# First chunk's diagonals by halves of 256 tokens, in a fused convolution and swish layer on one NeuronCore

## The chip, the cores and the metric

The kernel runs on one core of a Trainium2 chip. The metric is the device time of one execution in microseconds (us). Engines: PE is TensorE, with PEld its weight loads; DVE is VectorE; ACT is ScalarE; POOL is GpSimd; SP is SyncE, which here only issues DMAs.

## What is computed

```python
w = softmax(weight, axis=-1)                       # 8 heads x 7 taps
x_pad = zeros(6 tokens) ++ x                       # x: 8 x 4096 x 192, float32
a[b, s, h, g] = sum_k w[h, k] * x_pad[b, s + k, h, g]    # causal convolution, 24 channels a head
h = a.reshape(32768, 192) @ w_in                   # 192 x 2048
g = h * sigmoid(beta * h)                          # beta: 2048
out = g @ w_out                                    # 2048 x 192, float32
```

The kernel leaves the factor 1/beta to w_out: it computes silu(beta*h) and scales w_out's rows by 1/beta.

## The kernel before

**Tiling.** Channels lie on partitions, tokens along the free dimension. The 192 channels make three groups (index `c` or `j`, 0 to 2) of 64, and two batches are stacked, so a tile has 128 partitions: 64 channels of batch p and 64 of batch p+4. A chunk is 512 tokens (`TOK`), four blocks of 128; there are 32 chunks (`s`). `xt` is a chunk of x transposed, with a halo of earlier tokens in front; `ct` is the convolved chunk. For each chunk, 16 hidden blocks (`u` or `fc`) of 128 features follow: `hidden` multiplies w_in with ct on TensorE (L429), six matmuls of 64 rows, ScalarE applies silu (L437) into `g`. `output` (L511) multiplies g with w_out in pairs of matmuls (L465), accumulated over all 16 blocks in a PSUM tile; VectorE adds its two halves (L483), and SP writes them out.

**Order.** Each engine executes its instructions in the order in which the program issues them. The order is written by hand: what is called earlier stands earlier in its engine's queue. PSUM has three pools: `psum_h` with two buffers of two banks (tile `ph`), `psum_a` and `psum_b` with one each (`pa`, `pb`, from `in_a()` and `in_b()`). A new tile from a pool waits until the readers of the old one are done. Waits between engines follow from the tiles that instructions read and write.

**The start (chunk 0).** Weights and x are loaded in pieces by SP, ScalarE and POOL queues. `fill` (L215) issues matmuls of zeros whose result nobody reads. The softmax gives `cw`, the seven tap weights of each channel; `diags` (L255) makes diagonal matrices of them on VectorE, so that a tap of the convolution is a matmul with a diagonal. At L302 to L307 the four blocks b of chunk 0, cast to bf16 (L221), are transposed on TensorE (L228) and evacuated to `xt0`, by VectorE for b = 2 and by ScalarE for the others (L305); a fill follows b = 1 and b = 3. Then beta is transposed (L311) and copied (L312). At L340 the taps come as diagonal matmuls of 512 columns (`diag_tap`, L290): group 2 with three taps, group 0 with seven, group 1 with seven. VectorE adds the last four taps of group 2 (L328); ScalarE evacuates groups 0 and 1 (L345, L347), with the cast of w_in's first 256 columns between (L346), after it has cast half of the second chunk, `x1b` (L343).

**The second chunk.** `second()` (L365) transposes x1b with 24 small matmuls into a PSUM tile (L373), which VectorE copies to `xt1` and `xt` (L383). `conv1` (L394) makes group 0 of chunk 1 by diagonal matmuls at u = 4 and 5, evacuated by VectorE at u = 6 (L407); its other groups are VectorE's (L326, L328).

**Weights.** POOL issues w_in in quarters (L206). The last is issued after the first scaling of w_out on POOL (L316), which needs w_out's first quarter and `beta_r`, the reciprocal of beta (L359).

Of the kernel before, what the change touches and what calls it, by code (L numbers as in the profile page):

```python
# [9 lines left out]
FP32 = mybir.dt.float32  # L10
FP32R = mybir.dt.float32r
BF16 = mybir.dt.bfloat16
# [5 lines left out]
def kernel(  # L18
# [17 lines left out]
    nc = tc.nc  # L36

    B, S, D = x.shape
    H, K = weight.shape
    F = moe_w_in.shape[1]  # L40
    group = D // H
    DG = 64
    NG = D // DG
    HP = group // NG
    TOK = 512
    NF = F // 128
    PAD = K - 1
    HALO = 16
# [7 lines left out]
    NB = TOK // BLK  # L56
# [12 lines left out]
    psum_h = ctx.enter_context(  # L69
        tc.tile_pool(name="psum_h", bufs=2, space=bass.MemoryType.PSUM)  # L70
    )
# [9 lines left out]
    def in_a():  # L81
        return psum_a.tile([128, 2, TOK], FP32, name="pa")

    def in_b():
        return psum_b.tile([128, 2, TOK], FP32, name="pb")
# [25 lines left out]
    def new_xt(ch):  # L111
        xt = xt_pool.tile([128, NG, HALO + TOK], BF16, name="xt")
        xts[ch] = xt
        return xt
# [37 lines left out]
    beta_q = setup.tile([NF, 128], FP32)  # L152
# [15 lines left out]
    for r in range(2):  # L168
# [8 lines left out]
    xt0 = setup.tile([128, NG, HALO + TOK], FP32R)  # L177
# [9 lines left out]
        fill=0.0,  # L187
# [8 lines left out]
        fill=0.0,  # L196
# [18 lines left out]
    def fill(n, cols=TOK):  # L215
        zc = zeros.unsqueeze(1).to_broadcast((128, cols // 128, 128))
        for _ in range(n):
            nc.tensor.matmul(pf[:, 0, 0:cols], zeros, zc, start=True, stop=True)  # L218
# [36 lines left out]
    def diags(k0, k1):  # L255
        nc.vector.tensor_tensor(
            diag[:, k0:k1],
            ident.unsqueeze(1).to_broadcast((128, k1 - k0, 128)),
            cw[:, k0:k1].unsqueeze(2).to_broadcast((128, k1 - k0, 128)),
            ALU.mult,  # L260
        )
# [21 lines left out]
    cts = {}  # L283

    def new_ct(s):
        cts[s] = ct_pool.tile([128, NG, TOK], BF16, name="ct")

    def diag_tap(k, xt, pv, rows=slice(0, 128), k1=K):
        o = HALO - PAD + k
        nc.tensor.matmul(  # L290
            pv,
            diag[rows, k, :],
            xt[rows, o : o + TOK],
            start=(k == 0),
            stop=(k == k1 - 1),
        )
# [5 lines left out]
    for b in range(NB):  # L302
        pt = pts[b % 3][:, b // 3, 0 : NG * BLK].rearrange("p (c q) -> p c q", c=NG)
        transposes(pt, x0b, b)
        (nc.vector.tensor_copy if b == 2 else nc.scalar.copy)(tokens(xt0, b), pt)  # L305
        if b % 2:
            fill(1, 512 if b > 1 else 256)  # L307
    diags(2, 4)
    diags(4, K)
    pb = pf[:, 1, 0:NF]  # L310
    nc.tensor.transpose(pb, beta_q, ident[0:NF, 0:NF])  # L311
    nc.scalar.copy(beta, pb)  # L312

    def scale_w_out(i):
        fcs = slice(i * NQ, (i + 1) * NQ)
# [7 lines left out]
    def tap(dst, src, k, added):  # L323
# [6 lines left out]
            )  # L330


    new_ct(0)
    K_P = 3
    pvs = [
        psum_h.tile([128, 2, TOK], FP32, name="ph")[:, 0, :],
        in_b()[:, 0, :],
        in_a()[:, 0, :],
    ]
    for c, k1 in (2, K_P), (0, K), (1, K):  # L340
        for k in range(k1):
            diag_tap(k, xt0[:, c], pvs[c], k1=k1)
    for b in range(2):  # L343
        cast_rows(nc.scalar.copy, x1b, x1, b)
    nc.scalar.copy(cts[0][:, 0, :], pvs[0])  # L345
    nc.scalar.copy(w_in_s[:, :, 0:F0], w_in_raw)  # L346
    nc.scalar.copy(cts[0][:, 1, :], pvs[1])  # L347
    dst = cts[0][:, 2, :]
    for k in range(K_P, K):
        o = HALO - PAD + k  # L350
        tap(
            dst,
            xt0[:, 2, o : o + TOK].bitcast(FP32),
            k,
            pvs[2] if k == K_P else dst,
        )
    for b in range(2, NB):
        cast_rows(nc.vector.tensor_copy, x1b, x1, b)
# [3 lines left out]
    scale_w_out(1)  # L362


    def second():  # L365
        xt = new_xt(1)
        pt = in_b().bitcast(BF16)
        for b in range(NB):
            for c in range(NG):
                for r in range(2):  # L370
                    rows = slice(r * DG, (r + 1) * DG)
                    o = ((b // 2 * NG + c) * 2 + b % 2) * DG
                    nc.tensor.transpose(  # L373
                        pt[:, r, o : o + DG],
                        x1b[rows, b, c].rearrange("q h p -> q (h p)"),
                        ident_b[rows, rows],
                    )
        head, tail = slice(HALO - PAD, HALO), slice(HALO + TOK - PAD, HALO + TOK)
        nc.vector.tensor_copy(xt1[:, head], xt0[:, 0, tail])
        nc.vector.tensor_copy(xt[:, 1:, head], xt0[:, 1:, tail])  # L380
        for c in range(NG):
            dst = xt[:, c, HALO:] if c else xt1[:, HALO:]
            nc.vector.tensor_copy(  # L383
                dst.rearrange("p (i r q b) -> p i r q b", i=2, r=2, b=2),
                pt[:, :, 0 : NB * NG * DG].rearrange(
                    "p r (i c b q) -> p i r c q b", i=2, c=NG, b=2
                )[:, :, :, c],
            )
# [5 lines left out]
    def conv1(k0, k1):  # L394
        if not conv1_ps:
            new_ct(1)
            conv1_ps.append(in_b())
        pv = conv1_ps[0]
        for k in range(k0, k1):
            for r in range(2):  # L400
                diag_tap(k, xt1, pv[:, r, :], slice(r * DG, (r + 1) * DG))

    def conv1_evac():
        pv = conv1_ps[0]
# [16 lines left out]
    def hidden(s, fc, js=range(NG), ph=None, last=NG - 1):  # L421
        if fc == 0 and s not in gs:
            gs[s] = g_pool.tile([128, NF, 2, TOK], BF16, name="g")
        if ph is None:
            ph = psum_h.tile([128, 2, TOK], FP32, name="ph")
        for j in js:
            for h in range(2):
                rows = slice(h * DG, (h + 1) * DG)
                nc.tensor.matmul(  # L429
                    ph[:, h, :],  # L430
                    w_in_s[rows, j, fc * 128 : (fc + 1) * 128],
                    cts[s][rows, j, :],
                    start=(j == 0),
                    stop=(j == last),
                )
            if j == last:
                nc.scalar.activation(  # L437
                    gs[s][:, fc], ph, AF.Silu, scale=beta[:, fc : fc + 1]
                )
        return ph  # L440
# [70 lines left out]
    def output(s, u, pairs, free):  # L511
        for _ in range(pairs):
            for name in free:
                if slots[name] is None and waiting:
                    slots[name] = waiting.popleft()

            live = [(j.s, j.h, j.q, n) for n, j in slots.items() if j is not None]
            for *_, name in sorted(live):
                job = slots[name]
                if job.ready(s, u):  # L520
                    break
            else:
                return
            if job.po is None:
                job.po = place[name]()
            if job.pair():
                job.leave()
                slots[name] = None
# [22 lines left out]
    for s in range(N_ST):  # L551
        jobs_of(s)
        for u in range(NF):
            if s == 0 and u == min(CONV1):
                conv1(0, 2)
            if s > 0 or u > 2:
                hidden(s, u)
            elif u == 0:
                ph = hidden(0, 0, (0, 2), last=1)
                ph1 = hidden(0, 1, [0], last=1)  # L560
                hidden(0, 0, [1], ph, last=1)
                second()
                hidden(0, 1, (2, 1), ph1, last=1)
            elif u == 2:
                hidden(0, u, ph=in_a())
            if s > 0:
                n = 6 if s == N_ST - 1 else 4 if s == 1 and u == 0 else 8
                output(s, u, n, "ab")
            elif u > 7:
                output(s, u, 5 if u < NF - 1 else 10, "ab")  # L570
            elif u in QUOTA_A:
                output(s, u, QUOTA_A[u], "a")
            if s == 0:
                if u in CONV1:
                    conv1(*CONV1[u])
                if u == min(CONV1):
                    queue.extend(conv_ops(1, 1))
                for work in first_work.get(u, []):
                    (work or queue.popleft())()
            else:  # L580
                if u % 2 and queue and (s, u) != (1, 1):
                    queue.popleft()()

                if u == 0 and s + 3 < N_CH:
                    load(s + 3)
                if u < 2 and s + 2 < N_CH:
                    cast(s + 2, u)
                if u == 1 and s + 2 < N_CH:
                    xpose(s + 2)
                if (s, u) == (1, 1):  # L590
                    queue.popleft()()
            if u == 12 and s + 2 < N_CH:
                queue.extend(conv_ops(s + 2, 0))
# [32 lines left out]
```

## Time and profile before

| | us |
|---|---|
| median of 5 runs | 689.39 |
| lowest and highest | 689.14, 690.8 |
| the profiled execution: time | 690.8 |
| the profiled execution: span from first to last instruction | 689.0 |
| PE busy | 683.6 (99%) |
| ACT busy | 577.9 (84%) |
| DVE busy | 524.3 (76%) |
| POOL busy | 10.7 (2%) |

Times in the profile count from the span's start. A timeline row has start, length, engine, line, operation and tiles, and in square brackets the idle time of the engine before it with what ended the wait. Where a row stands for several instructions (x7), its length reaches from the first's start to the last's end. The end of a matmul is modelled and lies behind the start of the next; the pace is read from start to start.

### The profile page before, as it was taken

What the parts mean: (1) busy time and instruction counts of PE and PEld (TensorE: products, weight loads), DVE (VectorE), ACT (ScalarE), POOL (GpSimd) and SP (SyncE); (2) the same over time, 40 slices, a digit from 0 to 9 for tenths busy, and PEclk for the clock granted to TensorE, in tenths of its full rate; (3) what the DMA queues carried; (4) which work ended last, traced back from release to release, by engine and by line L of the source; (5) the groups of instructions that cost most, each with busy time, mean ns of one, the idle gap of its engine ahead of it and who ended that gap; (6) DMA issues with size and microseconds to landing.
All of it is one profiled execution on the core that took longest, in us unless ns stands there. A gap on an engine that the chain in (4) does not pass through costs nothing.

```text
span 689.0 us, 24342 instructions
## 1 busy us (share of the span) xinstructions
PE 683.6 (99%) x11312; PEld 520.2 (76%) x11312; DVE 524.3 (76%) x466; ACT 577.9 (84%) x529; POOL 10.7 (2%) x21
## 2 busy tenths in 40 slices
PE   9999999999999999999999999999999999999998
PEld 5777777777777777777777777777777777777777
DVE  6888877788777797777787777887777977777712
ACT  7888888888888888888888888888888888888893
POOL 4100000000000000000000000000000000000000
PEclk9999999999999999999999999999999999999999
DMA  9754332244332343332344332443324433322111
GB/s 232 178 110 117 105 99 85 64 116 116 94 104 67 88 116 105 100 103 56 104 117 105 95 85 67 116 117 93 105 65 89 117 106 99 97 62 59 49 36 59
DMA packets 121861, 67.06 MB, mean 97 GB/s; under 512 B 53264, under 2 KB 121760, under 8 KB 121760
## 3 DMA queue, kind: packets, MB, share of 16 engines
q1 hardware_dynamic: 120048, 64.12, 34.5%
q0 software_dynamic: 1664, 1.38, 1.2%
q8 instruction: 88, 1.44, 0.9%
q14 instruction: 13, 0.11, 0.0%
q10 hardware_dynamic: 48, 0.01, 0.0%
HBM read 29.89 MB, written 25.17 MB: 80 GB/s over the span
## 4 chain that ended last, share of the span: by engine, by line
PE 96%; DMA 3%; POOL 1%; DVE 0%; ACT 0%; issue 0%; POOLq 0%
PE ph L429 47%; PE pa L465 25%; PE pb L465 24%; DMA w_out_raw<-in_moe_w_out_dram 1%; DMA w_in_s<-in_moe_w_in_dram 1%; POOL w_in_s L206 0%; PE ph L218 0%; POOL w_out_s L316 0%; PE pa L239 0%; ACT cw L246 0%; ACT osb L481 0%; POOL hold L270 0%; DVE cw L249 0%; DVE nmax L245 0%; DVE total L248 0%
## 5 line engine op out<-in xcount | busy, mean ns | idle before, releaser
L437 ACT ACTIVATE g<-ph,beta 128x1024 bf16<-128x1024 f32 x511 | 568.5, 1114 | 95.4 <-PE ph L429 91.1
L465 PEld LDWEIGHTS <-g 64*128 64x128 bf16 x8160 | 369.9, 94 | 104.1 <-issue 0.9
L429 PE MATMUL ph<-ct,w_in_s 64*128 64x512 bf16 x3066 | 423.5, 376 | 0.2 <-DMA w_in_s<-in_moe_w_in_dram 0.2
L328 DVE SCALAR_TENSOR_TENSOR ct<-xt,cw,ct 128x1536 bf16<-128x1536 bf16 (+2 forms) x189 | 338.3, 1790 | 2.5
L465 PE MATMUL pa<-w_out_s,g 64*128 64x192 bf16 x4112 | 244.3, 243 | 0.1
L465 PE MATMUL pb<-w_out_s,g 64*128 64x192 bf16 (+1 forms) x4048 | 230.1, 243 | 0.3 <-DVE ct L407 0.3
L429 PEld LDWEIGHTS <-w_in_s 64*128 64x128 bf16 x3072 | 158.8, 94 | 54.7 <-issue 1.0
L483 DVE TENSOR_REDUCE osb<-pa 128x384 f32<-128x768 f32 x64 | 61.3, 958 | 122.9 <-PE pa L465 122.9
L483 DVE TENSOR_REDUCE osb<-pb 128x384 f32<-128x768 f32 x63 | 60.3, 958 | 29.0 <-PE pb L465 29.0
L106 DVE CAST xb<-xf 128x768 bf16<-128x768 f32 x60 | 40.6, 678 | 0.0
L326 DVE TENSOR_SCALAR ct<-xt,cw 128x1536 bf16<-128x1536 bf16 (+1 forms) x31 | 30.7, 990 | 0.0
L481 ACT COPY osb<-pb 128x192 f32<-128x192 f32 x1 | 0.3, 318 | 7.2 <-PE pb L465 7.2
L218 PE MATMUL ph<-zeros 128*128 128x512 bf16 (+2 forms) x10 | 4.5, 575 | 1.1 <-DVE warm L175 1.1
L206 POOL DMA_DIRECT2D w_in_s<-in_moe_w_in_dram x8 | 5.2, 657 | 0.0
L290 PE MATMUL pb<-xt,diag 64*128 64x512 f32 (+1 forms) x21 | 4.4, 437 | 0.3 <-DVE xt L383 0.3
L121 DVE COPY xt<-xt 128x18 bf16<-128x18 bf16 x27 | 4.4, 163 | 0.0
L316 POOL TENSOR_TENSOR w_out_s<-w_out_raw,beta_r 128x768 bf16<-128x768 f32 x2 | 3.9, 1926 | 6.7 <-DMA w_out_raw<-in_moe_w_out_dram 6.6
L290 PEld LDWEIGHTS pb<-xt,diag 64*128 64x128 f32 (+1 forms) x21 | 2.7, 187 | 1.3 <-PE ph L429 0.8
L218 PEld LDWEIGHTS <-zeros 128*128 128x128 bf16 x10 | 1.2, 134 | 2.2 <-issue 1.1
L176 ACT ACT_TABLE_LOAD x1 | 1.3, 1283 | 1.8 <-issue 1.8
L316 DVE TENSOR_TENSOR w_out_s<-w_out_raw,beta_r 128x768 bf16<-128x768 f32 x2 | 1.9, 943 | 0.0
L290 PE MATMUL ph<-xt,diag 128*128 128x512 f32 x7 | 1.8, 394 | 0.0
(59 smaller groups left out, 30.1 us busy)
## 6 DMA issues: line engine op xcount, KB each, us to landing
out_dram<-osb SPq DMA_DIRECT2D x127, 192.0 KB, 2.2
xf<-in_x_dram SPq DMA_DIRECT2D x60, 384.0 KB, 4.3
xt<-xb SPq DMA_TRANSPOSE x120, 2.5
x<-in_x_dram SPq DMA_DIRECT2D x4, 384.0 KB, 4.7
w_out_raw<-in_moe_w_out_dram SPq DMA_DIRECT2D x4, 384.0 KB, 11.3
w_in_s<-in_moe_w_in_dram POOLq DMA_DIRECT2D x6, 192.0 KB, 8.2
w_in_raw<-in_moe_w_in_dram SPq DMA_DIRECT2D x2, 192.0 KB, 6.7
w_in_s<-in_moe_w_in_dram POOLq DMA_DIRECT2D x2, 96.0 KB, 6.4
```

The lines of the kernel that those rows point to most:

```text
L106: nc.vector.tensor_copy(xbs[ch][:, :, :, h, :], xfs[ch][:, h].rearrange("q b (p c) -> q b c p", c=NG),)
L121: nc.vector.tensor_copy(dst, last[:, :, HALO + TOK - PAD :])
L206: nc.gpsimd.dma_start(out=w_in_s[r * DG : (r + 1) * DG, :, c0:c1], in_=w_in_v[:, :, c0:c1])
L218: nc.tensor.matmul(pf[:, 0, 0:cols], zeros, zc, start=True, stop=True)
L290: nc.tensor.matmul(pv, diag[rows, k, :], xt[rows, o : o + TOK], start=(k == 0), stop=(k == k1 - 1),)
L316: (nc.vector if i > 1 else nc.gpsimd).tensor_tensor(w_out_s[:, fcs, :], w_out_raw[:, fcs, :], beta_r[:, fcs].unsqueeze(2).to_broadcast((12 ...
L326: nc.vector.tensor_scalar_mul(dst, src, scalar)
L328: nc.vector.scalar_tensor_tensor(out=dst, in0=src, scalar=scalar, in1=added, op0=ALU.mult, op1=ALU.add)
L429: nc.tensor.matmul(ph[:, h, :], w_in_s[rows, j, fc * 128 : (fc + 1) * 128], cts[s][rows, j, :], start=(j == 0), stop=(j == last),)
L437: nc.scalar.activation(gs[s][:, fc], ph, AF.Silu, scale=beta[:, fc : fc + 1])
L465: nc.tensor.matmul(self.po[:, r, b * D : (b + 1) * D], g[rows, fc, self.h, q * BLK : (q + 1) * BLK], w_out_s[rows, fc, :], start=(self.don ...
L483: nc.vector.tensor_reduce(dst, self.po[:, :, 0 : nb * D].rearrange("p r n -> p n r"), axis=mybir.AxisListType.X, op=ALU.add,)
```

## The change

- The taps of groups 0 and 1 are made together, by halves of 256 tokens: one matmul has both groups' 256 tokens as its 2x256 columns. The order is four taps of half 0, three taps of group 2, three taps of half 0, seven of half 1. Half 0 goes to the unused second bank of the tile that took block 1's transposes.
- The evacuations change with it: half 0 for both groups in one copy, half 1 in two, one for each group.
- Beta's transpose and its copy, and `diags(2, 4)`, move to behind block 1's; both fills in the loop go.
- `second` is called in two parts: blocks 0 and 1 ahead of the first hidden matmuls, 2 and 3 where it was.
- PSUM pools a and b swap their roles for the second chunk's transposes, conv1, the hidden block u = 2 and the first output job.

```diff
-    def diag_tap(k, xt, pv, rows=slice(0, 128), k1=K):
-        o = HALO - PAD + k
+    def diag_tap(k, pv, moving, rows=slice(0, 128), k1=K):
         nc.tensor.matmul(
             pv,
             diag[rows, k, :],
-            xt[rows, o : o + TOK],
+            moving,
...
         (nc.vector.tensor_copy if b == 2 else nc.scalar.copy)(tokens(xt0, b), pt)
-        if b % 2:
-            fill(1, 512 if b > 1 else 256)
-    diags(2, 4)
+        if b == 1:
+            pb = pf[:, 1, 0:NF]
+            nc.tensor.transpose(pb, beta_q, ident[0:NF, 0:NF])
+            nc.scalar.copy(beta, pb)
+            diags(2, 4)
     diags(4, K)
-    pb = pf[:, 1, 0:NF]
-    nc.tensor.transpose(pb, beta_q, ident[0:NF, 0:NF])
-    nc.scalar.copy(beta, pb)
...
     K_P = 3
-    pvs = [
-        psum_h.tile([128, 2, TOK], FP32, name="ph")[:, 0, :],
-        in_b()[:, 0, :],
-        in_a()[:, 0, :],
-    ]
-    for c, k1 in (2, K_P), (0, K), (1, K):
-        for k in range(k1):
-            diag_tap(k, xt0[:, c], pvs[c], k1=k1)
+    HT = TOK // 2
+    halves = [pts[1][:, 1].bitcast(FP32), in_b()[:, 0, :]]
+    pv2 = in_a()[:, 0, :]
+
+    def half_taps(i, k0, k1):
+        for k in range(k0, k1):
+            o = HALO - PAD + i * HT + k
+            diag_tap(
+                k,
+                halves[i].rearrange("p (c t) -> p c t", c=2),
+                xt0[:, 0:2, o : o + HT],
+            )
+
+    def half_evac(i, c0, c1):
+        nc.scalar.copy(
+            cts[0][:, c0:c1, i * HT : (i + 1) * HT],
+            halves[i].rearrange("p (c t) -> p c t", c=2)[:, c0:c1],
+        )
+
+    half_taps(0, 0, 4)
+    for k in range(K_P):
+        o = HALO - PAD + k
+        diag_tap(k, pv2, xt0[:, 2, o : o + TOK], k1=K_P)
+    half_taps(0, 4, K)
+    half_taps(1, 0, K)
     for b in range(2):
         cast_rows(nc.scalar.copy, x1b, x1, b)
-    nc.scalar.copy(cts[0][:, 0, :], pvs[0])
+    half_evac(0, 0, 2)
     nc.scalar.copy(w_in_s[:, :, 0:F0], w_in_raw)
-    nc.scalar.copy(cts[0][:, 1, :], pvs[1])
+    half_evac(1, 0, 1)
+    half_evac(1, 1, 2)
...
-    def second():
-        xt = new_xt(1)
-        pt = in_b().bitcast(BF16)
-        for b in range(NB):
+    pt1 = in_a().bitcast(BF16)
+
+    def second(b0, b1):
+        pt = pt1
+        for b in range(b0, b1):
...
+        if b1 < NB:
+            return
+        xt = new_xt(1)
...
             elif u == 0:
+                second(0, 2)
                 ph = hidden(0, 0, (0, 2), last=1)
                 ph1 = hidden(0, 1, [0], last=1)
                 hidden(0, 0, [1], ph, last=1)
-                second()
+                second(2, NB)
                 hidden(0, 1, (2, 1), ph1, last=1)
             elif u == 2:
-                hidden(0, u, ph=in_a())
+                hidden(0, u, ph=in_b())
```

More of the change, by code (lines that the diff above doesn't have):

```diff
@@ L354 @@
             k,
-            pvs[2] if k == K_P else dst,
+            pv2 if k == K_P else dst,
         )
@@ L396, in conv1 @@
             new_ct(1)
-            conv1_ps.append(in_b())
+            conv1_ps.append(in_a())
         pv = conv1_ps[0]
         for k in range(k0, k1):
+            o = HALO - PAD + k
             for r in range(2):
-                diag_tap(k, xt1, pv[:, r, :], slice(r * DG, (r + 1) * DG))
+                rows = slice(r * DG, (r + 1) * DG)
+                diag_tap(k, pv[:, r, :], xt1[rows, o : o + TOK], rows)
     def conv1_evac():
@@ L571 @@
             elif u in QUOTA_A:
-                output(s, u, QUOTA_A[u], "a")
+                output(s, u, QUOTA_A[u], "b")
             if s == 0:
```

## The prediction

> **What bounds the kernel now.** I read the page's busy table first: TensorE is busy for 683.6 of 689.0 us, so only time that TensorE loses can be won, some 5 us in all, nearly all of it before 27 us. The change touches only the first 16 us; behind it the built program is the same instruction for instruction, but for two PSUM buffers that swap roles. So the question is which wait ends last between 0 and 27 us. The chain of waits that ended last, in order of time (start, length, what), answers it:
>
> ```profile
> 6.43 8.78 DMA w_out_raw<-in_moe_w_out_dram
> ...
> 15.38 1.49 POOL w_out_s L316
> 16.87 0.62 POOL w_in_s L206
> 17.49 8.49 DMA w_in_s<-in_moe_w_in_dram
> 25.98 0.05 issue
> 26.02 0.69 PE ph L429 x5
> ```
>
> The last quarter of w_in is queued on POOL behind the first scaling of w_out, which waits for a load; it lands at 25.98, and from then on TensorE runs without a gap. None of the taps, transposes or evacuations that the change edits is in this chain. The timeline (start, length, instruction, idle before it and its releaser) shows how near they are to it:
>
> ```profile
> 6.51 0.63 PE L218 MATMUL ph<-zeros 128*128 128x512 bf16 x1
> ...
> 6.75 0.51 ACT L305 CAST xt<-pb 128x384 fp32r<-128x384 bf16 x1 [0.41 <-PE pb L228]
> ...
> 7.31 1.13 PE L290 MATMUL pa<-xt,diag 128*128 128x512 f32 x3
> ...
> 8.28 1.79 PE L290 MATMUL ph<-xt,diag 128*128 128x512 f32 x7
> 8.57 0.75 DVE L328 SCALAR_TENSOR_TENSOR ct<-xt,cw,pa 128x512 bf16<-128x512 f32 x1 [0.79 <-PE pa L290]
> 9.35 2.33 DVE L328 SCALAR_TENSOR_TENSOR ct<-xt,cw,ct 128x512 bf16<-128x512 f32 x3
> ...
> 11.72 0.58 ACT L347 CAST ct<-pb 128x512 bf16<-128x512 f32 x1 [0.29 <-PE pb L290]
> ...
> 12.85 2.12 ACT L437 ACTIVATE g<-ph,beta 128x1024 bf16<-128x1024 f32 x2 [0.54 <-PE ph L429]
> ...
> 23.04 0.42 PE L465 MATMUL pb<-w_out_s,g 64*128 64x192 bf16 x6 [0.26 <-DVE ct L407]
> ...
> 25.40 0.38 PE L429 MATMUL ph<-ct,w_in_s 64*128 64x512 bf16 x1
> ...
> 26.02 0.82 PE L429 MATMUL ph<-ct,w_in_s 64*128 64x512 bf16 x5 [0.25 <-DMA w_in_s<-in_moe_w_in_dram]
> ```
>
> The two row halves of a hidden matmul run side by side. At u = 12 the first starts at 25.40 and its partner only at 26.02. So the front has **0.62 us of cover**: what it gains up to there is lost in this wait, and what it loses costs nothing until 0.62 us are used up.
>
> **The change, part by part**, on the times of this execution.
>
> Does the half start early? The new first matmul reads tokens of blocks 0 and 1 only (evacuated by 6.34). But in the built program it carries a wait for ScalarE's seventh count, which is the evacuation of block 3, and for VectorE's copy of block 2; the group that needs these blocks carries none of its own. Block 3's evacuation is the row at 6.75 and ends at 7.26. So the first tap starts at **7.31 as before**. The two fills go (0.21 and 0.43 us of columns at the cold rate) and leave TensorE idle from 6.6 to 7.31. Beta's transpose (0.28) and copy (0.17) move into ScalarE's idle 0.41 us before block 3: nothing. diags(2,4) ahead of block 2's copy shifts VectorE by 0.42 us at 6.2, inside waits: nothing.
>
> Taps: 17 before, 3+7+7; 17 after, 4+3+3+7. A tap of 2x256 columns is not in the trace: at least the 0.233 us from start to start of the 7 rows at 8.28 ((1.79-0.39)/6), at most twice a 256-column fill's pace, which is the same columns. I take 0.233. The third tap of group 2 comes four taps later: 8.05+4x0.233 = 8.98, and VectorE's first tap moves 8.57 to **9.50**, its fourth ends at 12.61 instead of 11.68. Half 0 is complete after ten taps, as group 0 was; its evacuation and the w_in cast stay at 10.11 and 10.59, and the last tap stays at 11.30. Half 1's two evacuations of 128x256 on ScalarE: between the 0.17 us of 16 columns and the 0.58 of 512, by width 0.37 each. c0 is then whole at 12.09 (10.69 before), c1 at about 12.4 (12.30).
>
> First hidden matmuls: before, the last pair started at 12.36, waiting for c1. After: j=0 at 12.1, j=2 waits for VectorE until 12.68, two more pairs of 0.216: 13.11. The first activation goes from 12.85 to **13.60**, and the next five stand back to back behind it, so ScalarE is 0.75 late until its seventh (19.24).
>
> Second chunk: 12 of the 24 transposes (0.17 of 0.34 us) run at 11.5 while TensorE waits anyway. The others follow the late hidden pair, 13.33 to 13.50 (x1b's cast, late with the taps, ends at 13.27). VectorE's copies move 13.14 to 13.72, **+0.58**. Behind them VectorE is busy without a break until conv1's evacuation; TensorE's wait for that (0.26 at 23.04) absorbs part of its lateness. TensorE, 0.65 behind and 0.26 of it regained, reaches u = 12 at about 25.8: 0.4 of the 0.62 is used. The end moves by 0.0 to 0.1. beta_r moves to 13.4, and w_out's scaling waits for its load until 15.23: 1.8 us of cover. SP's queue and POOL's keep their order.
>
> [...] POOL's scalings take 1.49 and 2.36 us for the same work, and in the same stretch three VectorE taps take 6.09 where others take 1.28 each. [...] Before, L326 (15.06 to 15.55) was ahead of the scaling at 15.38. [...] I take +0.1 for the end and keep -0.2 and +0.4 for the range.
>
> [...] The trace's clock record begins at 7.70 us; before, the fills start 0.43 us apart (1.89 for four at 1.06), later taps 0.233. [...] By the rows alone, the clock comes at 7.7 and the sum is +0.1. [...] nine taps at 0.427. Then the group-2 taps end the wait of VectorE at 10.65, its taps end at 13.76; the last tap starts at 12.79; the last hidden pair at 14.25 (+1.89); the first activation at 14.73; VectorE's copies at 14.86 (+1.73). TensorE is 1.8 late, regains the 0.26 at 23.04, and comes to u = 12 at 25.40+1.54 = 26.94 with no DMA left to wait for: its next pair at 26.96 instead of 26.02, **+0.94**. beta_r at 14.57 is still ahead of 15.23.
>
> **Rivals and their times.** The profiled execution was timed at 690.8 with a span of 689.0; the median of the runs is 689.39. I put the shift on the median. 0.2% of it is 1.38 us, about what can be told from no change.
>
> - The forecast: [...] no visible change, 689.39+0.94 = **690.3**. [...] Chance 0.40, its own range 689.9 to 690.7.
> - The clock on time, +0.1: 689.5, chance 0.29. For it: by instruction records TensorE is rarely idle; against it: the 0.7 us gap before 7.31.
> - The other side, slower: [...] From 11.1 on every us that it is late costs half a us, so +1.38 is reached at 12.0, and 13.4 gives +2.1. Place: TensorE's taps and first hidden matmuls, with no cover left. 691.1 in the middle, chance 0.25.
> - Earlier: [...] w_in lands 0.2 to 0.4 sooner, with the front no later than now: 689.1, chance 0.06. More can't come of it, since TensorE itself reaches u = 12 at 25.40. That the halves do start early (a wait ending at 6.6 instead of 7.31) is inside this: the gain would go into the same DMA wait.
>
> Slower than 0.2%: 0.25 of the third, some of the first's edge and of a later landing: 0.31. Faster: 0.03. The same: 0.66. The range 689.0 to 691.5 leaves out the ends of the third and fourth.
>
> **What would show it.** The first tap at 7.31 with nothing on TensorE for 0.7 us before it; VectorE's first tap at 9.5 (clock on time) or 10.6 (late); taps 0.43 apart beyond 7.7; the first activation at 13.6 or 14.7; the wait for w_in at u = 12 shrunk to 0.2 or gone; POOL's w_in issue within 0.4 of 16.87. I am wrong if the first tap starts near 6.6, if the load lands over 1 us away from 25.98, or if a difference arises behind 27 us.

## The result and the profile after

The changed kernel takes a median of 690.26 us over 22 runs (689.74 to 692.31), the kernel before 689.73 over 42 runs (689.10 to 691.0). The ratio is 1.0013 with a 95% interval of 1.0007 to 1.002: the change costs about 0.9 us. The medians alone differ by 0.53, the means (690.75 and 689.82) by 0.93, because the changed kernel's runs fall into two groups: 12 lie between 689.74 and 690.38, 10 between 691.35 and 692.31, and none between. The profiled execution is of the second group: 691.71 us with a span of 690.0, 1.0 more than the span before.

Its chain of waits (start, length, what) is shown from block 3's evacuation to the first output matmuls in PSUM pool a. It no longer holds a DMA:

```profile
6.74 0.52 ACT xt L304
...
7.30 2.08 PE ph L289 x4
9.38 1.29 PE pa L289 x3
...
10.77 0.76 DVE ct L326
...
13.93 0.82 PE ph L452 x6
14.76 0.19 PE pa L391 x12
...
14.97 1.90 DVE xt L404 x3
...
16.89 2.45 DVE ct L324
...
24.64 0.42 PE pa L488 x6
```

It goes from ScalarE's evacuation over the taps to VectorE's taps, from there over the first hidden matmuls and the second chunk's transposes to VectorE's copies, and through VectorE's queue to the output. The timeline of the same execution gives the rows that answer to those of before:

```profile
6.21 0.50 PE L228 MATMUL pb<-ident_b,x0b 128*128 128x128 bf16 x3
...
7.30 2.08 PE L289 MATMUL ph<-xt,diag 128*128 128x512 f32 x4 [0.60 <-ACT xt L304]
...
9.18 1.48 PE L289 MATMUL pa<-xt,diag 128*128 128x512 f32 x3
...
10.77 0.75 DVE L326 SCALAR_TENSOR_TENSOR ct<-xt,cw,pa 128x512 bf16<-128x512 f32 x1 [3.32 <-PE pa L289]
...
14.84 1.47 POOL L314 TENSOR_TENSOR w_out_s<-w_out_raw,beta_r 128x768 bf16<-128x768 f32 x1 [6.05 <-DVE beta_r L376]
14.85 2.12 ACT L460 ACTIVATE g<-ph,beta 128x1024 bf16<-128x1024 f32 x2 [1.18 <-PE ph L452]
14.97 0.69 DVE L404 CAST xt<-pa 128x512 fp32r<-128x512 bf16 x1 [0.18 <-PE pa L391]
...
24.64 0.42 PE L488 MATMUL pa<-w_out_s,g 64*128 64x192 bf16 x6 [0.17 <-DVE ct L430]
...
27.00 0.83 PE L452 MATMUL ph<-ct,w_in_s 64*128 64x512 bf16 x6
```

Read the first tap: it starts at 7.30 as before, released by ScalarE's block 3, and TensorE is idle for 0.60 us ahead of it. Read then the pace: four taps from 7.30 to the next group at 9.18 is 0.47 each, and three from 9.18 to 10.46 is 0.43 each, where before the third tap was already followed after 0.23. The trace's clock record (the stretch in which TensorE was granted its full clock) begins at 10.57 instead of 7.70; from 10.75 on the taps are 0.23 apart here too. At u = 12 (the last row) six matmuls start at 27.00 with no wait for the w_in load; before, the first stood at 25.40 and the rest at 26.02. So TensorE is 0.98 later from there on, which is the difference of the spans. Nothing arises behind this point: in all fourteen profiles of this document, 661.9 to 662.1 us lie between the first hidden matmul of u = 13 and the end.

### The profile page after: what moved, and what is told of

Its sections match the earlier page's. It is cut to its first block, busy times and chain, and to the rows that moved or that the text cites. A ratio compares the mean times of both kernels' runs of the same rounds, so it can differ in the third digit from the quotient of the medians.

```text
span 690.0 us, 24339 instructions
## 1 busy us (share of the span) xinstructions
PE 684.2 (99%) x11310; PEld 519.9 (75%) x11310; DVE 524.0 (76%) x466; ACT 577.7 (84%) x530; POOL 9.8 (1%) x21
## 4 chain that ended last, share of the span: by engine, by line
PE 97%; DVE 2%; ACT 0%; issue 0%; DVEq 0%
PE ph L452 47%; PE pb L488 24%; PE pa L488 24%; DVE ct L326 1%; PE ph L218 0%; DVE ct L324 0%; PE ph L289 0%; DVE xt L404 0%; DVE ct L430 0%; PE pa L289 0%; PE pb L228 0%; PE pa L239 0%; ACT xt L304 0%; PE pa L228 0%; PE ph L228 0%
## 5 line engine op out<-in xcount | busy, mean ns | idle before, releaser
L326 DVE SCALAR_TENSOR_TENSOR ct<-xt,cw,ct 128x1536 bf16<-128x1536 bf16 (+2 forms) x189 | 336.2, 1779 | 2.5
L488 PE MATMUL pb<-w_out_s,g 64*128 64x192 bf16 x4112 | 243.6, 243 | 0.0
L488 PE MATMUL pa<-w_out_s,g 64*128 64x192 bf16 (+1 forms) x4048 | 229.7, 243 | 0.2 <-DVE ct L430 0.2
L324 DVE TENSOR_SCALAR ct<-xt,cw 128x1536 bf16<-128x1536 bf16 (+1 forms) x31 | 32.6, 1052 | 0.0
L218 PE MATMUL ph<-zeros 128*128 128x512 bf16 (+1 forms) x8 | 3.5, 588 | 1.1 <-DVE warm L175 1.1
L289 PE MATMUL pa<-xt,diag 64*128 64x512 f32 (+1 forms) x17 | 4.2, 489 | 0.2 <-DVE xt L404 0.2
L326 DVE SCALAR_TENSOR_TENSOR ct<-xt,cw,pa 128x512 bf16<-128x512 f32 x1 | 0.7, 748 | 3.3 <-PE pa L289 3.3
L289 PEld LDWEIGHTS pa<-xt,diag 64*128 64x128 f32 (+1 forms) x17 | 2.4, 212 | 1.1 <-PE ph L452 0.6
L289 PEld LDWEIGHTS ph<-xt,diag 128*128 128x128 f32 x7 | 1.9, 294 | 1.3 <-ACT xt L304 0.9
```

The lines of the kernel that those rows point to most:

```text
L289: nc.tensor.matmul(pv, diag[rows, k, :], moving, start=(k == 0), stop=(k == k1 - 1),)
L324: nc.vector.tensor_scalar_mul(dst, src, scalar)
L326: nc.vector.scalar_tensor_tensor(out=dst, in0=src, scalar=scalar, in1=added, op0=ALU.mult, op1=ALU.add)
L488: nc.tensor.matmul(self.po[:, r, b * D : (b + 1) * D], g[rows, fc, self.h, q * BLK : (q + 1) * BLK], w_out_s[rows, fc, :], start=(self.don ...
```

## The experiments

There are two theories: **the clock** (the lost fills and the gap ahead of the first tap make TensorE's full clock come later) and, as rival, **the order** (group 2 later, half 1's evacuations late). Besides ratio and median, two numbers are read from each list of runs: the fastest run, and how many lie above 691.2 us, where the changed kernel's upper group begins.

**The fills put back.** An `if b % 2: fill(1, 512 if b > 1 else 256)` behind the `if b == 1` block of the changed kernel's loop.

> The changed kernel with both fills put back behind blocks 1 and 3. Theory (the lost fills make the clock late): the clock record begins near 7.7 instead of 10.57, taps are 0.233 us apart from the second or third on, VectorE's first tap is at 9.5, the first activation at 13.6, VectorE's copies of the second chunk at 13.7, and the wait for w_in at u = 12 is back; time +0.0 to +0.1 us on the kernel before. Rival (the new order of the taps is what costs): the time stays near the changed kernel's, +0.5 to +0.9, though the clock comes early.

Measured: ratio 1.0012 (1.0003 to 1.0022), fastest run 690.23, 9 of 14 above 691.2; the clock record begins at 10.84. On its face this is the rival's result, but the timeline shows that the fill did not fill:

```profile
5.66 0.28 PE L307 MATMUL ph<-ident,beta_q 16*128 16x16 f32 x1
6.45 0.37 PE L218 MATMUL ph<-zeros 128*128 128x256 bf16 x1 [0.51 <-ACT beta L308]
6.62 0.53 PE L228 MATMUL pa<-ident_b,x0b 128*128 128x128 bf16 x3
...
8.06 0.79 PE L289 MATMUL ph<-xt,diag 128*128 128x512 f32 x1 [0.17 <-ACT xt L304]
```

Beta's transpose went to the fills' PSUM tile, so the next fill waits until ScalarE has copied beta; the transposes and the taps behind it are 0.7 us late. This run therefore decides nothing between the two theories.

**The kernel before without its two fills** (the `if b % 2: fill(...)` deleted).

> The kernel before without the two fills behind blocks 1 and 3, nothing else changed. Theory: the clock comes at 10 to 11.1, ten taps or so are 0.43 us apart, the last tap moves from 11.3 to about 12.8, the first activation from 12.85 to about 14.2, and the time grows by about 0.5 us (VectorE's first tap moves by 0.4 only, since group 2 is still first). Rival (order of the taps): the clock may come late, but the time is that of the kernel before within 0.1.

Measured: 1.0007 (0.9997 to 1.0018), fastest 689.11, 5 of 14 above 691.2. The profiled execution contradicts the expectation: its clock came at 6.82, ahead of the first tap, and from the second tap on all are 0.23 apart. So the missing fills do not make the clock late in every execution; with 5 of 14 above 691.2 beside 5 of 51 of the kernel before, they seem to change the odds. The ratio means about +0.5 us, as expected (the medians differ by 0.75), but its interval holds 1.

**Group 2 first, no fills.**

```diff
-    half_taps(0, 0, 4)
     for k in range(K_P):
         o = HALO - PAD + k
         diag_tap(k, pv2, xt0[:, 2, o : o + TOK], k1=K_P)
-    half_taps(0, 4, K)
+    half_taps(0, 0, K)
```

> The changed kernel with group 2's three taps ahead of half 0's; no fills. Theory: the clock is as late as in the changed kernel, VectorE's first tap is back at 9.1 to 9.3 instead of 10.77, and the chain over VectorE's taps and copies no longer ends last; the activations are still about 1.3 late behind the late last tap, so the time stays +0.3 to +0.7 on the kernel before. Rival (order of the taps): the time is that of the kernel before within 0.1.

Measured: 1.0014 (1.0003 to 1.0025), fastest 689.47, 8 of 14 above 691.2; clock at 10.87, VectorE's first tap at 9.06. Group 2's place is worth 0.27 us in the fastest runs (689.74 to 689.47), and nothing that can be seen in the ratio. The upper group stays, so it does not come from group 2's place.

**The load of w_in's last quarter early, in the kernel before.**

```diff
-    scale_w_out(0)
     load_w_in((NW - 1) * FW, F)
+    scale_w_out(0)
     scale_w_out(1)
```

> The kernel before with the load of w_in's last quarter issued on POOL ahead of the first scaling of w_out instead of behind it. Theory (0.62 us of cover in the wait at u = 12): the load is issued at about 8.8, lands well before 25, the wait at u = 12 is gone, and the time falls by 0.4 to 0.6 us. If another load is pushed back by it (w_out's quarters, the next x chunk), a new wait takes its place and less is won. If the wait at u = 12 is not what ends last: no change.

Measured: 0.9991 (0.9985 to 0.9998), about 0.6 us less, fastest 689.12, none of 21 above 690.5. The wait for w_in is gone, but the fastest run is as fast as that of the kernel before (689.09): the wait seems to bind in some executions only.

**The fills put back without the wait** (the first ahead of beta's transpose).

```diff
         if b == 1:
+            fill(1, 256)
             pb = pf[:, 1, 0:NF]
...
+        if b == 3:
+            fill(1, 512)
     diags(4, K)
```

> The changed kernel with both fills put back, the first ahead of beta's transpose, so that it does not wait for beta's copy. Two parts are now told apart: the fastest runs (clock early; the changed kernel 689.74, the kernel before 689.1) show what the order of taps and evacuations costs[...]. Theory: the fastest runs stay at 689.7 to 689.8, and at most 2 of 14 lie above 691.2; median 690.2 to 690.5. Rival (the fills do nothing for the clock): 5 to 8 of 14 above 691.2, median near 691.3.

Measured: **1.0001 (0.9993 to 1.001)**, median 690.25 (before, in the same comparison: 690.16), fastest 689.73, 1 of 13 above 691.2. With nothing but two fills of zeros added, the ratio is no longer clear of 1 and one run of the upper group is left. Its profiled execution had the clock at 6.94, and shows the changed order with the clock on time:

```profile
7.50 1.20 PE L289 MATMUL ph<-xt,diag 128*128 128x512 f32 x4 [0.30 <-ACT xt L304]
...
9.50 0.75 DVE L329 SCALAR_TENSOR_TENSOR ct<-xt,cw,pa 128x512 bf16<-128x512 f32 x1 [1.85 <-PE pa L289]
...
13.58 2.12 ACT L463 ACTIVATE g<-ph,beta 128x1024 bf16<-128x1024 f32 x2 [1.18 <-PE ph L455]
13.70 0.69 DVE L407 CAST xt<-pa 128x512 fp32r<-128x512 bf16 x1 [0.17 <-PE pa L394]
...
25.40 0.83 PE L455 MATMUL ph<-ct,w_in_s 64*128 64x512 bf16 x6
```

At u = 12 (the last row) its six matmuls start at 25.40, 1.60 ahead of the changed kernel's 27.00.

**The same with group 2 first** (both edits).

> The same with group 2's three taps first. Theory: fastest runs at 689.3 to 689.5 (in the run of group 2 first without fills 689.47), at most 2 of 14 above 691.2, median 689.9 to 690.3, so within 0.05% of the kernel before. Rival (the lateness of group 2 is not what the fastest runs show): fastest runs at 689.75.

Measured: 1.0001 (0.9993 to 1.0009), median 690.11, fastest 689.48, 1 of 13 above 691.2. In its profile the clock came at 4.57, the earliest of all, and yet its span is 689.0, as before the change, for this reason:

```profile
25.34 0.38 PE L454 MATMUL ph<-ct,w_in_s 64*128 64x512 bf16 x1
26.00 0.61 PE L454 MATMUL ph<-ct,w_in_s 64*128 64x512 bf16 x4 [0.28 <-DMA w_in_s<-in_moe_w_in_dram]
```

That is the wait of before again: what the front wins is lost at u = 12 when w_in lands late (25.96 here, 25.98 before).

**The halves apart.** xt0 becomes two parts in a row, each with its own halo, so that half 0's taps conflict with no write of blocks 2 and 3. (An extract; the other places that index xt0 are changed to match.)

```diff
-    xt0 = setup.tile([128, NG, HALO + TOK], FP32R)
+    xt0 = setup.tile([128, 2, NG, HALO + HT], FP32R)
...
             diags(2, 4)
+            nc.vector.tensor_copy(
+                xt0[:, 1, :, HALO - PAD : HALO],
+                xt0[:, 0, :, HALO + HT - PAD :].bitcast(FP32),
+            )
...
-                xt0[:, 0:2, o : o + HT],
+                xt0[:, i, 0:2, o : o + HT],
```

> The changed kernel with the two halves of chunk 0 stored one behind the other, each with its own halo, so that a tap of half 0 waits only for blocks 0 and 1. No fills. Theory: the first tap starts at 6.5 instead of 7.30 with no gap ahead of it, [...] at most 3 of 14 runs above 691.2; VectorE's first tap about 0.3 to 0.7 earlier than in the changed kernel at the same clock; fastest runs 689.1 to 689.5. Rival (the wait for block 3 costs nothing): as the changed kernel, 689.75 and half of the runs above 691.2.

Measured: 1.0000 (0.9992 to 1.0008), fastest 688.97, 1 of 13 above 691.2. The first tap follows the transposes without a gap (no idle time in its row):

```profile
6.43 0.50 PE L229 MATMUL pb<-ident_b,x0b 128*128 128x128 bf16 x3
6.69 0.78 PE L289 MATMUL ph<-xt,diag 128*128 128x512 f32 x1
```

This second way of keeping TensorE busy, with no fill in it, also takes the ratio back to 1. Together, the four kernels with the gap filled (the last three and the next) have 3 of 52 runs above 691.2.

**The halves apart with the early load.**

> The same with w_in's last quarter loaded ahead of w_out's first scaling. Theory: fastest runs as in the run without it (the wait for w_in does not bind when the clock is early), the slow ones gain, none above 691.0; median 689.5 to 689.8, 0.05 to 0.1% below the kernel before. If the load is not what the slow runs wait for: as the run without it.

Measured: 1.0003 (0.9994 to 1.0011), median 690.29, fastest 689.01, slowest 690.95. No run lies above 691.0, as expected, but the forecast gain in the median is missing: no gain over the halves alone can be seen.

**No fill after the first four, in the kernel before** (`fill(3)` and `fill(1, 128)` behind the softmax's matmul deleted too).

> The kernel before without any fill after the first four: neither the fills behind the softmax's matmul nor those behind blocks 1 and 3. Theory: TensorE is now idle from 3.4 to 4.9 and from 6.5 to 7.3, [...] the clock comes after 10 in nearly every execution. At least 10 of 14 runs above 690.8 us (the kernel before: 4 to 10 in 50), none under 690.0, median 691.3 to 691.8. Rival (the clock comes by chance, whatever TensorE does): the spread of the kernel before, some runs at 689.1.

Measured: **1.0018 (1.0012 to 1.0025)**, 690.71 to 692.05, 17 of 21 above 690.8; clock at 11.34. The median of 691.37 lies where it was expected, and none of the runs is near 689.1, which the rival needed. The more TensorE idled ahead of the taps, the more runs were late: by its waits from 5 us to the first tap in the profiles, 0.54 us in the kernel before without its two fills (5 of 14 runs above 691.2), 0.60 in the changed kernel (10 of 22) and with group 2 first (8 of 14), 0.68 with the fills put back (9 of 14), 2.33 here (14 of 21). Of the kernels whose fills are gone or stuck behind a wait (this one, the changed kernel, and the first three experiments), 46 of 85 runs lie above 691.2; of the kernel before, 8 of 192 over all comparisons.

**One part alone: the split transposes**, with the early load.

> The kernel before with w_in's last quarter loaded early and one part of the change alone: the second chunk's transposes in two parts, with the PSUM pools swapped. Theory: the first 12 transposes fill time in which TensorE waits for ScalarE, and 0.17 us less stands behind the first hidden matmuls; VectorE's copies start about 0.1 earlier; 0 to 0.15 us on the kernel with the early load alone. Rival: the part costs something (a wait for the other pool): slower than the early load alone by 0.2 or more.

Measured: 0.9996 (0.9987 to 1.0004), median 690.01 beside 689.91 of the early load alone on the same chip. These runs can tell neither the small gain nor a cost.

**The early load again.**

> The kernel before with the early load alone, again, beside the other two on the same chip. Theory: 0.05 to 0.13% below the kernel before, no run above 690.9. Rival (the first result was the luck of the clock): no difference.

Measured: 0.9998 (0.999 to 1.0006), one run at 690.97 where none above 690.9 was expected. The gain of the first result did not show again; the two together do not settle whether the early load is a gain.

**More fills ahead of the taps.** The early load, `fill(1, 128)` behind the first four fills, and `fill(1, 256)` for the `fill(1, 128)` ahead of the transposes.

> The kernel before with the early load and 256 columns of fills more, in two gaps of TensorE ahead of the taps: 128 behind the first four fills (2.74 to 2.88 is idle) and 128 before the first transposes (4.76 to 4.90). [...] Theory: [...] the clock always comes by 7.7; no run above 690.5, median 689.2 to 689.7, 0.05 to 0.12% below the kernel before. Rival ([...] the fills delay the softmax's matmul): the spread of the early load alone, 689.1 to 691.0, or slower.

Measured: 0.9998 (0.999 to 1.0007), median 689.49 (before, in the same comparison: 689.74), fastest 689.2, one run at 690.85; clock at 4.66. The median is where it was expected, the difference is not clear of zero, and one run breaks the stated bound. The first added fill was not free: the softmax's matmul starts at 2.99 instead of 2.88, and the fastest run is 0.1 slower. So no kernel here beats the one before beyond doubt.

## Why the prediction was right, and where not

**The clock.** The forecast was nine taps at 0.427 from 7.31 on, so a full clock after about 11.15, and +0.94 us. That it would be just nine was not shown by the trace of the kernel before. The profiled execution went through the forecast's steps: the clock at 10.57, VectorE's first tap at 10.77 (10.65), the first activation at 14.85 (14.73), VectorE's copies at 14.97 (14.86), the matmul at u = 12 at 27.00 (26.96), the span +1.0. That the clock came 0.58 ahead of the forecast did not matter to this chain, since group 2's last tap, which VectorE waits for, was followed by the next tap at 10.46, ahead of both. Putting fills back, or closing the gap in another way, takes the ratio to 1.0001 and 1.0000, and taking more fills out of the kernel before raises its ratio from 1.0007 to 1.0018. That TensorE's idle time ahead of the taps brings the upper group of runs is shown, not only argued. The table has the start of the clock record and the time of the same execution:

| kernel | clock, us | time, us |
|---|---|---|
| before | 7.70 | 690.8 |
| changed | 10.57 | 691.71 |
| fills put back, stuck | 10.84 | 691.92 |
| before without fills | 6.82 | 690.25 |
| group 2 first | 10.87 | 691.28 |
| before, early load | 9.45 | 690.5 |
| fills without wait | 6.94 | 690.12 |
| fills, group 2 first | 4.57 | 690.7 |
| halves apart | 8.72 | 690.19 |
| halves apart, early load | 5.25 | 689.73 |
| no late fills | 11.34 | 691.33 |
| split, early load | 9.63 | 690.42 |
| early load again | 9.36 | 690.97 |
| more fills | 4.66 | 690.12 |

The four executions whose clock came after 10.5 took 691.28 to 691.92 us; the ten whose clock came by 9.7 took 689.73 to 690.97. This is from these fourteen executions alone. What sets the moment of the clock within one kernel is not shown: it came at 4.57 in one and at 9.45 in another kernel that gives TensorE the same instructions up to 4.57.

**What the forecast had too simple** is the late clock as the typical case. The upper group of the changed kernel's runs is taken for the late clock, since all fourteen profiles divide that way; the clock of a run without a profile was not recorded. If so, the clock is late in 10 of 22 executions, and these cost about twice the forecast: their mean of 691.79 is 1.97 above that of the kernel before (689.82), while the lower group's, 689.89, is 0.07 above it. Neither group stands at +0.94; the mean of +0.93 is their mixture. That the median of 690.26 meets the forecast of 690.3 is luck: it lies between the two slowest runs of the lower group, and the forecast put +0.94 on 689.39, where the kernel before has 689.73 over its 42 runs. The +0.94 came from a late clock's 1.54 at u = 12 less the wait for w_in there. The 1.54 was right (27.00 beside 25.40 is 1.60, in the profiles of the kernel before and of the fills without wait alike); the wait, as the next paragraph says, is not there in every execution. The rival "on the other side" (+1.4 to +2.1) has about the size of the upper group, but its reason, a clock after 12.0, was not seen: the latest in any trace is 11.34.

**The clock on time, +0.1**, holds on average (+0.07 for the lower group, a ratio of 1.0001 with the fills back) but not for the fastest runs. Its steps were right up to the second chunk, as the kernel with the fills back shows: VectorE's first tap at 9.50 (predicted 9.50), the first activation at 13.58 (13.60), the copies at 13.70 (13.72), though its taps start at 7.50. TensorE then came to u = 12 at 25.40, not at 25.8: it was only 0.25 late at 23.03, which the wait for VectorE there (0.26 before, none now) absorbed. The term that failed is the cover of 0.62 us: it belongs to executions in which w_in lands late. POOL's first scaling, behind which that load is issued, started at 15.38 in the kernel before and at 13.84 with the fills back, both waiting for w_out's load; w_in landed at 25.98 and at 24.55. Where it lands early nothing covers the front. I take this for the reason why the fastest runs of the changed order (689.73) are 0.63 us slower than those of the kernel before (689.10); 0.25 of it is group 2's later place (689.48), the rest was not told apart, and no profile shows an execution as fast as these.

**The first tap at 7.31** was right (7.30), and with it that the halves do not start early; the halves apart, at 6.69, show that the wait for block 3 was the reason.

**beta_r** was expected ahead of w_out's load at 15.23. It came at 14.70, as predicted (14.57), but the load was there before it: POOL waited for VectorE, the row at 14.84. It cost nothing, as no DMA wait was left at u = 12. The issue of w_in came 0.57 earlier than before (16.25 for 16.82), more than the 0.4 that the prediction allowed; the load landed at 25.79, 0.19 ahead of before.

**POOL and VectorE.** POOL's two scalings took 1.47 us each in the changed kernel; what took longer there was VectorE's L324:

```profile
16.25 1.29 POOL L206 DMA_DIRECT2D w_in_s<-in_moe_w_in_dram  x2
16.89 2.44 DVE L324 TENSOR_SCALAR ct<-xt,cw 128x1024 bf16<-128x1024 bf16 x1
...
17.56 1.47 POOL L314 TENSOR_TENSOR w_out_s<-w_out_raw,beta_r 128x768 bf16<-128x768 f32 x1
```

In this timeline of the changed kernel it takes 2.44 us where 0.49 was its row before, and ends 0.3 after POOL's scaling. In the kernel before without its two fills, it starts inside a scaling and also ends 0.3 after it:

```profile
14.81 1.47 POOL L314 TENSOR_TENSOR w_out_s<-w_out_raw,beta_r 128x768 bf16<-128x768 f32 x1 [6.00 <-DMA w_out_raw<-in_moe_w_out_dram]
14.89 1.67 DVE L324 TENSOR_SCALAR ct<-xt,cw 128x1024 bf16<-128x1024 bf16 x1
```

In three more profiles it starts inside a scaling (group 2 first, the early load, the halves apart): it takes 1.71, 1.08 and 0.67 us there and ends 0.29, 0.28 and 0.27 after it. By what it is held up was not shown. Nor is it settled why it took so long in the changed kernel, where it started during the issue of w_in and 0.67 ahead of the scaling: in the first experiment it started during the same issue and took 0.49. VectorE's chain lost 1.95 us here and gave TensorE the 0.17 of wait at 24.64; TensorE was about as late by itself.

## What to carry to other kernels

Look at what TensorE does ahead of its first long run of matmuls: here even work whose result nobody reads counted. Deleting it or stalling it behind a wait left 46 of 85 runs above 691.2 us, and with the gap filled it was 3 of 52; it changes how often an execution is slow, not by how much each is. Read the lists of runs as well as a profile, since one profile shows one draw of such odds, and a wait that covers a loss in it need not be there in the next. A median can meet a forecast because it is the edge of one group of runs. A fill must not share a tile with anything that is read: the wait that it gets (0.51 us in the first experiment) stalls what it was to keep busy.

## Not expected

- With the fills in place the clock came anywhere from 4.57 to 9.63 us after the first instruction. In the kernel before without its two fills it came at 6.82 in the one execution profiled, ahead of the 7.70 with them.
- w_out's first quarter, issued at 6.4 to 6.6 in every execution, let POOL's scaling start at 13.27 in one (group 2 first, no fills) and at 15.38 in another (before), both waiting for that load: a spread of 2.1 us whose cause stays open.
- A VectorE instruction (L324, L326 before) that took 0.49 us in the kernel before took 1.67 in the kernel before without its two fills, where it started inside a scaling on POOL, and 2.44 in the changed kernel.
